# Five edits to the order of work in a recurrent attention segment: second scores moved up, tAB transposed in halves, fill transposed at the segment boundary, vA evacuated ahead of pS, one shared Wo pair traded for a Wv pair

## The chip, the cores and the metric

The kernel runs on one core of one Trainium2 chip. The metric is the device time of one execution in microseconds. The kernel before was timed three times.

## The reference

Two branches read the same `x` (2048 rows of 1024). Branch A is an attention with a small memory that is carried from segment to segment: 64 segments of 32 rows, 8 memory rows, 32 heads of 128. Branch B is a feed-forward block. A sigmoid gate mixes the two.

```
mem = mem0
for s in range(64):
    h = concat(mem, x[32*s : 32*s+32])                 # 40 rows x 1024
    q, k, v = h @ Wq, h @ Wk, h @ Wv                   # 32 heads of 128
    p = softmax(where(mask, q k^T / sqrt(128), -1e9))  # 40 x 40 a head
    o = (p v) @ Wo                                     # 40 x 1024
    mem = o[:8];  out[32*s : 32*s+32] = o[8:]
b = (gelu(x @ w_gate) * (x @ w_up)) @ w_down
return g * a + (1 - g) * b,   g = sigmoid((x * gate_w).sum(-1))
```

The memory rows make the segments a chain: segment s+1 cannot project its memory before Wo of segment s is done.

## The kernel before

The first three quarters of the time are the 64 segments, the rest is branch B, which the change leaves alone.

**Weights.** Each of Wq, Wk, Wv, Wo is cut into 16 pieces of 512 KB: 8 pieces (`i`) for each half of the heads (`u`). There is room for 50 of the 64 pieces. `PAIRS` names the indices whose two pieces (u = 0 and u = 1) share one slot; these 14 slots are loaded again in each segment, the others stay. `spent(k)` says that a piece has been used for the last time in the order of the walk, and issues the next load into its slot on SyncE's queue (SP). All reloads of a segment go through this one queue: first two Wk, two Wq and four Wv pieces near the start of the segment, then six Wo pieces during the first Wo pass. Wo pieces are read in strided form at first; `keep` writes them once into `wo_scr`, from where later loads are straight.

**Walk.** A segment is a fixed list of steps `(m, r, n)`: matrix m, round r (0 or 1, the half of the heads), place n. `HEAD` holds the first halves of k, q and v with pieces of the last Wo pass of the segment before in between; `BODY` is k, q of round 1, Wo of round 0 (`"o", 0`), v of round 1, and the first four Wo pieces of round 1 (`"o", 1`). `plan(s)` hangs all other work on these steps with `on(m, r, n, f)`; `f` runs ahead of that step. Each engine has one queue, which is worked off in the order in which `plan` and the walk emit it; waits are put in by a tracker of tiles (`_Prog`), which treats a PSUM bank as one thing and SBUF in cells of 64 bytes. Tiles share memory on purpose: stage `p` lies over `oRc` and `a_bf`, stage `q` over `qT`, `tAB` and `E8`, and `vA` and stage `o` over `oT`.

**One attention half.** `scores(u)` (PE lines 647 and 653, then DVE 659, 660, ACT 661, DVE 663 to 672) ends with the transpose `tAB` on DVE (line 672). `attend(u)` (PE lines 681 and 686) multiplies it with `vA`, the evacuated v. `take` copies the four result banks into `oT`, which Wo (line 735 in round 0, line 752 in round 1) reads. `trans` transposes a staged k or q on PE (`turn`, line 631, always into bank TT) and copies it back on DVE (line 617).

**Boundary.** `fold` (DVE lines 763, 764) adds the halves of Wo's result into `a_bf`, `next_mem` transposes this on PE (line 773) and copies it on DVE (line 776) into `hT`, the input of the next segment. `a_bf` is then written to `a_scr` by a DMA issued on GpSimd (POOL). PE is kept busy across the boundary by a fill or by `warm`, matmuls without a use.

**Fills.** Eight rows of each segment do not depend on the memory, so k, q and v of these rows are computed for four segments at once (`fill`, lines 789 and 799). `FILL` says which: after segments with s % 4 = 0 a k and a q, 1 a v and a q, 2 a v, 3 a k; they end with s = 58. A k or q fill is evacuated, transposed with `turn`, copied on DVE (line 821), and written to `qk_scr` by POOL (line 824). All writes to `qk_scr` share one lane, so each waits for the landing of the one before.

**Around the change.** In a segment s > 0 before, the first scores stand at `("k", 1, 0)`; ScalarE evacuates k of round 1 into stage `p` (`pS`, at `("q", 1, 1)`) and then v into `vA` (at `("q", 1, 3)`). At `("o", 0, 0)` stand the first `attend`, into banks B0, B1, B2 and SS, the transpose of `pS`, the q evacuation and the four takes (all on DVE); the second scores stand at `("o", 0, 6)`.

Of the kernel before, what the change touches and what calls it, by code (L numbers as in the profile page):

```python
# [210 lines left out]
def bass_gated_mix__memory_aug_recurrent_mem_tr__geglu_ffn__prompt_kernel(  # L211
# [34 lines left out]
    with ExitStack() as es:  # L246
# [133 lines left out]
        def keep(k):  # L380
# [5 lines left out]
        moved = {("o", 0, i): slots[home[h]] for i, h in zip(PAIRS["o"], (("k", 1, 2), ("k", 1, 3), ("k", 1, 4),  # L386
                                                                          ("q", 1, 6), ("q", 1, 7), ("v", 1, 4)))}
        nlane = [0]
# [238 lines left out]

        def turn(st):
            def f(e):
                for j in range(4):  # L630
                    ins = e.transpose(PBV[TT][:, j * 128:(j + 1) * 128], st[:, j * 128:(j + 1) * 128], ident[:, :])  # L631
                return ins
            op("pe", f, rd=[st.r(), ident.r()], wr=[BK(TT)])

        def trans(to, st):
            turn(stage[st])
            dve_copy(to[:, :, :, 0:32].rearrange("p j g c -> p (j g) c"),
                     PBV[TT][:, 0:512].rearrange("p (j g c) -> p (j g) c", g=4, c=32), [BK(TT)], [to.r()])

# [4 lines left out]
        def scores(u):  # L644

            def f(e):
# [24 lines left out]
               rd=[E8.r(), st8.r(8, 16)], wr=[pAB.r(256)])  # L671
            op("dve", lambda e: e.transpose(tAB[:, :], pAB[:, 0:512]), rd=[pAB.r()], wr=[tAB.r()], after=[fin])

        def attend(u, by=((2, "act"), (3, "dve"), (0, "act"), (1, "dve"))):
            bo = (B0, B1, B2, SS)

            def f(e):
                for j in range(4):
                    for g in range(4):
                        r = slice(32 * g, 32 * g + 32)  # L680
                        e.matmul(PB[bo[g]][:, j * LQ:(j + 1) * LQ], lhsT=vA[r, j, :],
                                 rhs=tAB[r, 64 * j:64 * j + LQ],
                                 start=(j == 0), stop=False, skip_group_check=True)
# [11 lines left out]
        def take(by):  # L695
            n = 4 * LQ
            for g, eng in by:
                b = (B0, B1, B2, SS)[g]
                cp[eng](oT[:, g, :, :].rearrange("p j c -> p (j c)"), PB[b][:, 0:n], [BK(b)], [oT.r(g * n, (g + 1) * n)])
# [8 lines left out]
        def proj(s, m, r, n):  # L708
# [14 lines left out]
            elif r == 0:  # L723
# [91 lines left out]

        def fill_put(m, u, G, st):
            if m == "v":
                return
            st = stage[st]
            turn(st)  # L820
            op("dve", lambda e: e.tensor_copy(st[:, :].rearrange("p (i x c) -> p x i c", i=4, x=16),
                                              PBV[TT][:, 0:512].rearrange("p (x i c) -> p x i c", x=16, i=4)), rd=[BK(TT)], wr=[st.r()])
            m4 = 3 * u if m == "q" else 1 + u
            op("pool", lambda e: e.dma_start(qk_scr[:, 4 * G:4 * G + 4, m4, :], st[:, :].rearrange("p (i y) -> p i y", i=4)),
               rd=[st.r()], wr=[("D", "qk", G, m, u)], lane="fq")
# [14 lines left out]
        def some(fs, n):  # L840
            return lambda: run(fs, n)
# [6 lines left out]
        def plan(s):  # L848
# [8 lines left out]
            def on(m, r, n, *fs, s=s):  # L857
                at.setdefault((s, m, r, n), []).extend(fs)

            if s == 0:  # L860
# [12 lines left out]
                on("k", 0, 4, gate)  # L873
                on("k", 0, 5, lambda: (firsts("v", 1), firsts("o", 0), firsts("o", 1)))
            if s % 4 == 3 and G < NG:
# [16 lines left out]
            if s == 0:  # L892
                on("k", 1, 1, lambda: attend(ua))
# [214 lines left out]
```

## Time and profile before

| | |
|---|---|
| runs (3) | 2383.08, 2384.80, 2384.88 us, median 2384.8 |
| profiled execution | 2371.4 us, span 2369.6 us |
| mean granted TensorE clock | 0.983 |
| PE busy | 2130.4 us, 90% of the span |
| DVE busy | 1044.7 us, 44% |
| ACT busy | 519.1 us, 22% |
| POOL busy | 432.9 us, 18% |
| DMA moved | 639.42 MB, mean 270 GB/s |

A segment takes some 25 us in the profile: segment 32 begins with its k projection at 927.27 us and the next at 952.75 us. The busy share of PE is a mean over stages and counts overlapping matmuls once, so what counts below is where PE stands idle inside a segment, and what ended that wait. The profiled execution was 13.4 us faster than the median of the runs.

### The profile page before, as it was taken

How to read it: one execution, taken by the hardware profiler on the slowest of the kernel's cores; microseconds unless marked ns; L12 is line 12 of the kernel's file. 1: busy time of each engine (PE TensorE's matmuls, PEld its weight loads, DVE VectorE, ACT ScalarE, POOL GpSimd, SP SyncE). 2: the span in 40 equal slices, each digit the busy share in tenths (PEclk: the TensorE clock that was granted, in tenths of full speed). 3: DMA queues.
4: the chain of work that ended last, by engine and by line, in shares of the span. 5: the costliest groups of instructions: out<-in, count | busy, mean ns of one | idle time of the engine just before them, and what ended most of it. 6: DMA issues, size and time to landing. Idle time of an engine off the chain costs nothing.

```text
span 2369.6 us, 74769 instructions
## 1 busy us (share of the span) xinstructions
PE 2130.4 (90%) x33827; PEld 1054.9 (45%) x33852; DVE 1044.7 (44%) x2438; ACT 519.1 (22%) x985; POOL 432.9 (18%) x821
## 2 busy tenths in 40 slices
PE   4588888989999998999899989988899999999999
PEld 2244444444444444444444444444464444444444
DVE  3344444444444444444444444444415436264463
ACT  1122222222222222222222222222103213032130
POOL 4322222222222222212222222222100000000000
PEclk9799999999999999999999999999999999999999
DMA  9979999989999999999899989999976260713530
GB/s 374 349 267 315 326 321 329 333 309 320 322 316 322 319 323 314 324 324 322 307 321 326 312 318 326 323 318 330 336 249 200 76 217 10 249 53 101 174 99 18
DMA packets 261453, 639.42 MB, mean 270 GB/s; under 512 B 28264, under 2 KB 102760, under 8 KB 261136
## 3 DMA queue, kind: packets, MB, share of 16 engines
q1 hardware_dynamic: 237312, 597.66, 72.4%
q0 software_dynamic: 13888, 26.31, 3.5%
q10 hardware_dynamic: 9936, 10.69, 1.3%
q8 instruction: 266, 4.36, 0.7%
q14 instruction: 51, 0.42, 0.0%
HBM read 596.85 MB, written 37.68 MB: 268 GB/s over the span
## 4 chain that ended last, share of the span: by engine, by line
PE 48%; DMA 29%; DVE 8%; issue 7%; ACT 5%; POOL 3%; ACTq 0%; SPq 0%; POOLq 0%
DMA a_scr<-a_bf 16%; PE pb L1009 14%; DMA wall<-wo_scr 6%; PE pb L719 6%; PE pb L1063 6%; PE pb L735 5%; PE pb L752 3%; PE pb L789 3%; DMA wall<-in_A_Wo_dram 2%; PE pb L960 2%; PE pb L1044 2%; PE pb L631 2%; PE pb L799 2%; ACT pS L614 1%; DMA xr_scr<-xr 1%
## 5 line engine op out<-in xcount | busy, mean ns | idle before, releaser
L719 PE MATMUL pb<-sl,hT 128*32 128x512 bf16 x12288 | 770.1, 382 | 7.2 <-issue 5.0
L719 PEld LDWEIGHTS pb<-sl,hT 128*32 128x32 bf16 x12288 | 342.4, 97 | 273.7 <-DVE hT L776 21.7
L789 PE MATMUL pb<-sl,hR 128*32 128x512 bf16 x3072 | 224.0, 393 | 9.2 <-issue 8.3
L1009 PE MATMUL pb<-xT,wg 128*128 128x512 bf16 x896 | 211.7, 379 | 0.7
L1009 PE MATMUL pb<-xT,wu 128*128 128x512 bf16 x896 | 211.7, 379 | 0.0
L752 PE MATMUL pb<-wall,oT 128*32 128x256 bf16 x4048 | 152.1, 276 | 38.0 <-DMA wall<-wo_scr 16.5
L763 DVE COPY part<-pb 64x256 f32<-64x256 f32 x128 | 54.0, 422 | 265.9 <-PE pb L752 263.4
L735 PE MATMUL pb<-wall,oT 128*32 128x512 bf16 x2048 | 153.1, 396 | 7.6 <-issue 0.2
L614 ACT ACTIVATE kS<-pb 128x512 bf16<-128x512 f32 x127 | 75.8, 597 | 367.9 <-PE pb L719 349.2
L617 DVE CAST oT<-pb 128x160 bf16<-128x160 f32 x382 | 105.5, 318 | 110.3 <-PE pb L686 110.3
L702 POOL COPY oRc<-oT 128x128 bf16<-128x128 bf16 x128 | 96.2, 752 | 313.3 <-DVE oT L617 311.9
L661 ACT ACTIVATE E<-pb 128x320 bf16<-128x320 f32 x128 | 56.0, 437 | 428.1 <-DVE pb L660 428.1
L1063 PE MATMUL pb<-wd,GT 128*128 128x512 bf16 x657 | 144.9, 379 | 2.1 <-DMA wd<-in_B_w_down_dram 1.2
L752 PEld LDWEIGHTS pb<-wall,oT 128*32 128x32 bf16 x4048 | 97.7, 97 | 93.8 <-issue 36.8
L1009 PEld LDWEIGHTS pb<-xT,wg 128*128 128x128 bf16 x896 | 87.0, 98 | 108.1 <-DVE GT L1025 3.7
L1017 ACT ACTIVATE s<-pb 128x512 f32<-128x512 f32 x112 | 66.7, 596 | 311.6 <-PE pb L1009 311.6
L1009 PEld LDWEIGHTS pb<-xT,wu 128*128 128x128 bf16 x896 | 87.5, 98 | 105.9
L1018 DVE SCALAR_TENSOR_TENSOR tp<-s,pb 128x512 f32<-128x512 f32 x112 | 77.0, 687 | 124.1 <-ACT s L1017 123.9
L659 DVE TENSOR_REDUCE st<-pb 128x8 f32<-128x320 f32 x128 | 62.9, 492 | 137.5 <-PE pb L653 137.5
L617 DVE COPY kT<-pb 128x512 bf16<-128x512 bf16 x128 | 53.7, 420 | 156.6 <-PE pb L631 156.6
L828 POOL COPY kT<-qkr 128x128 bf16<-128x128 bf16 x128 | 37.3, 291 | 451.6 <-DVE kT L617 389.3
L789 PEld LDWEIGHTS pb<-sl,hR 128*32 128x32 bf16 x3072 | 84.7, 99 | 68.6 <-issue 20.9
(93 smaller groups left out, 2249.9 us busy)
## 6 DMA issues: line engine op xcount, KB each, us to landing
wall<-wo_scr SPq DMA_DIRECT2D x336, 512.0 KB, 6.9
sl<-in_A_Wv_dram SPq DMA_DIRECT2D x268, 512.0 KB, 10.8
sl<-in_A_Wk_dram SPq DMA_DIRECT2D x142, 512.0 KB, 5.7
sl<-in_A_Wq_dram SPq DMA_DIRECT2D x142, 512.0 KB, 8.4
wd<-in_B_w_down_dram SPq DMA_DIRECT2D x42, 1024.0 KB, 5.5
wall<-in_A_Wo_dram SPq DMA_DIRECT2D x52, 512.0 KB, 7.9
wdF<-in_B_w_down_dram SPq DMA_DIRECT2D x7, 1024.0 KB, 7.7
wo_scr<-wall SPq DMA_DIRECT2D x12, 512.0 KB, 11.9
```

What stands on the lines that cost most here:

```text
L614: op("act", lambda e: e.activation(o, i, ACTF.Copy), rd=rd, wr=wr)
L617: op("dve", lambda e: e.tensor_copy(o, i), rd=rd, wr=wr)
L659: op("dve", lambda e: e.tensor_reduce(nm, sS, AX.X, ALU.max, negate=True), rd=[BK(SS)], wr=[st8.r(0, 8)])
L702: op("pool", lambda e: e.tensor_copy(oRc[:, :, 16 * u:16 * u + 16].rearrange("p c x -> p x c"), oT[:, :, :, 32:40].rearrange("p g j c -> p ...
L719: ins = e.matmul(PB[bk][32 * g:32 * g + 32, :], lhsT=h[:, i, :], rhs=w[:, g * 512:(g + 1) * 512], start=(n == 0), stop=(n == 7))
L735: ins = e.matmul(PB[XO][32 * g:32 * g + 32, :], lhsT=oT[:, j, x, 0:32], rhs=wall[:, na:nb + 1:nb - na, c:c + 256], start=(n == 0 and hp == 0),
L752: ins = e.matmul(PB[XO][32 * g:32 * g + 32, 256 * b:256 * b + 256], lhsT=oT[:, j, x, 0:32], rhs=w[:, c:c + 256], start=False, stop=(n % 4 ...
L789: ins = e.matmul(PB[b][32 * g:32 * g + 32, :], lhsT=h[:, k[2], :], rhs=w[:, g * 512:(g + 1) * 512], start=(n == 0), stop=(n == 7))
L1009: ins = e.matmul(PB[bk][:, 0:FB], lhsT=w[:, kc, cc:cc + 128], rhs=xT[:, :, :, kc, :].rearrange("p t i c -> p (t i) c"), start=(kc == 0), s ...
L1017: op("act", lambda e, hg=hg: e.activation(s1[:, :], hg, ACTF.Square, scale=SQ), rd=[BK(bg)], wr=[s1.r()])
L1018: op("dve", lambda e, hg=hg, t=t: e.scalar_tensor_tensor(out=t[:, :], in0=s1[:, :], scalar=1.0, in1=hg, op0=ALU.add, op1=ALU.mult), rd=[BK ...
L1063: ins = e.matmul(PB[bank[2 * k + hf]][:, :], lhsT=GT[:, j, tb * 128:(tb + 1) * 128], rhs=w[:, jj, hf * 512:(hf + 1) * 512], start=(j == 0) ...
```

## The change

- **Pairs.** Wo index 7 loses its shared slot and stays resident; Wv index 4 gets one. There are still 14 reloads in a segment: 2 Wk, 2 Wq, 5 Wv, 5 Wo. The fifth Wv reload is issued when piece 4 of v has been used in `HEAD`. The release of Wo slots in round 0 is spread differently (piece 0 after place 1; 1, 4 and 5 after place 3; 6 after place 5), and round 1 uses its pieces in the order 2, 3, 0, 1, 7, 4, 5, 6.
- **vA ahead of pS.** `vA` is evacuated at `("k", 1, 4)`. The first `attend` writes bank A0 in place of SS, its takes go to DVE (0, 3) and ACT (1, 2).
- **First scores** move from `("k", 1, 0)` to `("v", 0, 7)`, and the q transpose ahead of them goes one piece up, into bank A0. **Second scores** move from `("o", 0, 6)` to `("o", 0, 4)`, with their q transpose in bank SS.
- **tAB in halves.** The transpose of 512 columns becomes two of 256; `attend` becomes two operations, the first of which waits for the first half only.
- **Fill turned at the boundary.** The first fill of a segment is staged in `q` rather than `k`, its four transposes move from `("o", 1, 2)` to behind `fold(s, 0)`, into bank SS, and its DVE copy and its write to `qk_scr` to behind `next_mem(s, 0)`.

```diff
-        PAIRS = {"k": (0, 1), "q": (0, 1), "v": (0, 1, 2, 3), "o": (0, 1, 4, 5, 6, 7)}
+        PAIRS = {"k": (0, 1), "q": (0, 1), "v": (0, 1, 2, 3, 4), "o": (0, 1, 4, 5, 6)}
...
+            if m == "o":
+                return sorted(f + p, key=lambda i: i // 4)
...
-            op("dve", lambda e: e.transpose(tAB[:, :], pAB[:, 0:512]), rd=[pAB.r()], wr=[tAB.r()], after=[fin])
+            for c in (0, 256):
+                op("dve", lambda e, c=c: e.transpose(tAB[:, c:c + 256], pAB[:, c:c + 256]), rd=[pAB.r(c, c + 256)], wr=[tAB.r(c, c + 256)], after=[fin])
...
-            bo = (B0, B1, B2, SS)
+            bo = (B0, B1, B2, b3)
...
-            op("pe", f, rd=[vA.r(), tAB.r(), vB.r()], wr=[BK(b) for b in bo])
+            op("pe", f, rd=[vA.r(), tAB.r(0, 256)], wr=[BK(b) for b in bo])
+            op("pe", f2, rd=[tAB.r(256), vB.r()], wr=[BK(b) for b in bo])
...
-                    spent((*k[:2], i - 4))
-                    spent(k)
+                    for x in {1: (0,), 3: (1, 4, 5), 5: (2, 6), 7: (3, 7)}[n]:
+                        spent((*k[:2], x))
...
+        def fill_turn(m, st, bank=TT):
+            if m != "v":
+                turn(stage[st], bank)
+
-        def fill_put(m, u, G, st):
+        def fill_put(m, u, G, st, bank=None):
...
-            on("v", 0, 6, lambda: trans(qT, "q"))
+            on("v", 0, 5 if s else 6, lambda: trans(qT, "q", A0 if s else TT))
+            if s > 0:
+                on("v", 0, 7, lambda: scores(ua))
...
-            on(*(("k", 1, 1) if s == 0 else ("q", 1, 3)), lambda: evac(bank_of["v", 0], vA, "act"))
-            on("k", 1, 1 if s == 0 else 0, lambda: scores(ua))
+            on("k", 1, 1 if s == 0 else 4, lambda: evac(bank_of["v", 0], vA, "act"))
...
-                on("o", 0, 0, lambda: attend(ua, ((0, "dve"), (1, "dve"))))
-            on("o", 0, 0, lambda: trans(kT, "p" if s else "k"))
-            on("o", 0, 0, lambda: put_rest())
-            on("o", 0, 0, lambda: evac(bank_of["q", 1], stage["q"], "act"))
-            if s > 0:
-                on("o", 0, 0, lambda: take(((2, "dve"), (3, "dve"))))
-                on("o", 0, 0, lambda: rest_o(ua))
-            on("o", 0, 2, lambda: trans(qT, "q"))
-            on("o", 0, 6, lambda: scores(ub))
+                on("o", 0, 0, lambda: attend(ua, ((0, "dve"),), A0))
+                on("o", 0, 0, lambda: evac(bank_of["q", 1], stage["q"], "act"))
+                on("o", 0, 0, lambda: trans(kT, "p"))
+                on("o", 0, 0, lambda: put_rest())
+                on("o", 0, 0, lambda: take(((1, "act"), (2, "act")), A0))
+                on("o", 0, 2, lambda: trans(qT, "q", SS))
+                on("o", 0, 2, lambda: take(((3, "dve"),), A0))
+                on("o", 0, 2, lambda: rest_o(ua))
+                on("o", 0, 4, lambda: scores(ub))
...
-                on("o", 1, 0, lambda: fill_evac(*fl[0], A1, "k"))
-                on("o", 1, 2, lambda: fill_put(*fl[0], "k"))
+                on("o", 1, 0, lambda: fill_evac(*fl[0], A1, "q"))
...
             on("k", 0, 0, lambda: fold(s, 0), **nx)
+            if fl:
+                on("k", 0, 0, lambda: fill_turn(fl[0][0], "q", SS), **nx)
             on("k", 0, 0, some(f2, 4) if two else lambda: warm(5), **nx)
             on("k", 0, 0, lambda: next_mem(s, 0), **nx)
+            if fl:
+                on("k", 0, 0, lambda: fill_put(*fl[0], "q", SS), **nx)
```

More of the change, by code (lines that the diff above doesn't have):

```diff
@@ L626, in evac, with turn, trans @@
                 cp[how](t[:, :], PB[bank][:, :], [BK(bank)], [t.r()])
-        def turn(st):
+        def turn(st, bank=TT):
             def f(e):
                 for j in range(4):
-                    ins = e.transpose(PBV[TT][:, j * 128:(j + 1) * 128], st[:, j * 128:(j + 1) * 128], ident[:, :])
+                    ins = e.transpose(PBV[bank][:, j * 128:(j + 1) * 128], st[:, j * 128:(j + 1) * 128], ident[:, :])
                 return ins
-            op("pe", f, rd=[st.r(), ident.r()], wr=[BK(TT)])
-        def trans(to, st):
-            turn(stage[st])
+            op("pe", f, rd=[st.r(), ident.r()], wr=[BK(bank)])
+        def trans(to, st, bank=TT):
+            turn(stage[st], bank)
             dve_copy(to[:, :, :, 0:32].rearrange("p j g c -> p (j g) c"),
-                     PBV[TT][:, 0:512].rearrange("p (j g c) -> p (j g) c", g=4, c=32), [BK(TT)], [to.r()])
+                     PBV[bank][:, 0:512].rearrange("p (j g c) -> p (j g) c", g=4, c=32), [BK(bank)], [to.r()])
         sS = PB[SS][:, 0:320].rearrange("p (a c) -> p a c", a=8)
@@ L671, in scores, with attend @@
                rd=[E8.r(), st8.r(8, 16)], wr=[pAB.r(256)])
[L672 to L675 removed]
+            for c in (0, 256):
+                op("dve", lambda e, c=c: e.transpose(tAB[:, c:c + 256], pAB[:, c:c + 256]), rd=[pAB.r(c, c + 256)], wr=[tAB.r(c, c + 256)], after=[fin])
+        def attend(u, by=((2, "act"), (3, "dve"), (0, "act"), (1, "dve")), b3=SS):
+            bo = (B0, B1, B2, b3)
             def f(e):
@@ L680, in f, with f2 @@
                         r = slice(32 * g, 32 * g + 32)
-                        e.matmul(PB[bo[g]][:, j * LQ:(j + 1) * LQ], lhsT=vA[r, j, :],
-                                 rhs=tAB[r, 64 * j:64 * j + LQ],
-                                 start=(j == 0), stop=False, skip_group_check=True)
+                        ins = e.matmul(PB[bo[g]][:, j * LQ:(j + 1) * LQ], lhsT=vA[r, j, :],
+                                       rhs=tAB[r, 64 * j:64 * j + LQ],
+                                       start=(j == 0), stop=False, skip_group_check=True)
+                return ins
+            def f2(e):
                 for g in range(4):
@@ L693, in attend, with take @@
                 rest_o(u)
-        def take(by):
+        def take(by, b3=SS):
             n = 4 * LQ
             for g, eng in by:
-                b = (B0, B1, B2, SS)[g]
+                b = (B0, B1, B2, b3)[g]
                 cp[eng](oT[:, g, :, :].rearrange("p j c -> p (j c)"), PB[b][:, 0:n], [BK(b)], [oT.r(g * n, (g + 1) * n)])
@@ L814, in fill_evac @@
                 act_copy(st[:, :], PB[b][:, :], [BK(b)], [st.r()])
-        def fill_put(m, u, G, st):
+        def fill_turn(m, st, bank=TT):
+            if m != "v":
+                turn(stage[st], bank)
+        def fill_put(m, u, G, st, bank=None):
             if m == "v":
@@ L819, in fill_put @@
             st = stage[st]
-            turn(st)
+            if bank is None:
+                bank = TT
+                turn(st)
             op("dve", lambda e: e.tensor_copy(st[:, :].rearrange("p (i x c) -> p x i c", i=4, x=16),
-                                              PBV[TT][:, 0:512].rearrange("p (x i c) -> p x i c", x=16, i=4)), rd=[BK(TT)], wr=[st.r()])
+                                              PBV[bank][:, 0:512].rearrange("p (x i c) -> p x i c", x=16, i=4)), rd=[BK(bank)], wr=[st.r()])
             m4 = 3 * u if m == "q" else 1 + u
@@ L901, in plan @@
             if s > 0:
-                on("o", 0, 0, lambda: attend(ua, ((0, "dve"), (1, "dve"))))
-            on("o", 0, 0, lambda: trans(kT, "p" if s else "k"))
-            on("o", 0, 0, lambda: put_rest())
-            on("o", 0, 0, lambda: evac(bank_of["q", 1], stage["q"], "act"))
-            if s > 0:
-                on("o", 0, 0, lambda: take(((2, "dve"), (3, "dve"))))
-                on("o", 0, 0, lambda: rest_o(ua))
-            on("o", 0, 2, lambda: trans(qT, "q"))
-            on("o", 0, 6, lambda: scores(ub))
+                on("o", 0, 0, lambda: attend(ua, ((0, "dve"),), A0))
[7 more added lines that the diff above has]
+                on("o", 0, 4, lambda: scores(ub))
+            else:
+                on("o", 0, 0, lambda: trans(kT, "k"))
+                on("o", 0, 0, lambda: put_rest())
+                on("o", 0, 0, lambda: evac(bank_of["q", 1], stage["q"], "act"))
+                on("o", 0, 2, lambda: trans(qT, "q"))
+                on("o", 0, 6, lambda: scores(ub))
             on("v", 1, 0, some(f1, 3))
```

6 lines of the change are left out of this document (4 added, 2 removed).

## The prediction

> **What bounds the kernel now.** I read the page first, then the waits over the stretch 200 to 1715 us, which holds 60 of the 64 segments, then the order in time inside segment 32.
>
> ```profile
> PE 2130.4 (90%) x33827; PEld 1054.9 (45%) x33852; DVE 1044.7 (44%) x2438; ACT 519.1 (22%) x985; POOL 432.9 (18%) x821
> ...
> DMA a_scr<-a_bf 16%; PE pb L1009 14%; DMA wall<-wo_scr 6%; PE pb L719 6%; PE pb L1063 6%; PE pb L735 5%; PE pb L752 3%; PE pb L789 3%; DMA wall<-in_A_Wo_dram 2%; PE pb L960 2%; PE pb L1044 2%; PE pb L631 2%; PE pb L799 2%; ACT pS L614 1%; DMA xr_scr<-xr 1%
> ```
>
> The first line is of the page's engines, the second of its chain by line. PE is 90% busy, so only its idle tenth can be won. The chain runs 16% of the span through the small write of `a_bf` to `a_scr`, but what that write costs is only the part during which PE has nothing left to do. The waits say how much that is (columns: who waited for whom, us in total, times, longest):
>
> ```profile
> ACT pS L614 <- DMA a_scr<-a_bf: 92.0, 59, 3.6
> PE pb L681 <- ACT vA L614: 44.4, 54, 2.9
> PE pb L681 <- DVE tAB L672: 23.0, 48, 1.7
> PE pb L752 <- DMA wall<-wo_scr: 15.6, 27, 1.1
> ```
>
> Four places recur: the first attend (behind vA, itself behind pS, itself behind `a_scr`), the second attend (behind the transpose of tAB), Wo pieces that come late, and, in the rows below, the transpose of a staged fill between two groups of Wo. Each has one edit aimed at it. Segment 32 in time (start, duration, in brackets the idle time before it and what ended it):
>
> ```profile
> 939.41 0.60 ACT L614 ACTIVATE pS<-pb 128x512 bf16<-128x512 f32 x1 [2.31 <-DMA a_scr<-a_bf]
> 939.91 0.59 ACT L614 ACTIVATE vA<-pb 128x512 bf16<-128x512 f32 x1
> 940.55 0.27 PE L681 MATMUL pb<-tAB,vA 32*128 32x40 bf16 x16 [1.57 <-ACT vA L614]
> 942.28 1.05 PE L735 MATMUL pb<-wall,oT 128*32 128x512 bf16 x16
> 943.26 0.31 PE L647 MATMUL pb<-mS,ident 128*128 128x320 bf16 x1
> 944.79 1.93 PE L719 MATMUL pb<-sl,hT 128*32 128x512 bf16 x32
> 946.87 0.71 DVE L672 STREAM_TRANSPOSE tAB<-pAB 128x512 bf16<-128x512 bf16 x1
> 947.86 0.28 PE L681 MATMUL pb<-tAB,vA 32*128 32x40 bf16 x16 [0.49 <-DVE tAB L672]
> 948.60 0.62 PE L752 MATMUL pb<-wall,oT 128*32 128x256 bf16 x16
> 949.42 0.40 PE L631 MATMUL pb<-ident,kS 128*128 128x128 bf16 x4 [0.20 <-ACT kS L614]
> 949.75 0.40 PE L752 MATMUL pb<-wall,oT 128*32 128x256 bf16 x8
> 950.55 1.05 PE L789 MATMUL pb<-sl,hR 128*32 128x512 bf16 x16
> ...
> 951.25 0.42 DVE L764 TENSOR_TENSOR a_bf<-pb,part 64x256 bf16<-64x256 f32 x1
> 951.72 0.23 PE L773 MATMUL pb<-ident,a_bf 64*128 64x64 bf16 x2
> ```
>
> **A, vA ahead of pS.** Today the first attend starts 1.14 us after pS starts (939.41 to 940.55), because vA follows on the same queue, 0.50 us later. With vA done before, attend may follow pS itself, since it now writes bank A0, which pS has to empty first: the wait for `a_scr` stays, 0.50 us of it goes. The 54 waits total 44.4 us, mean 0.82, so most are longer than 0.50; at most 54 x 0.50 = 27 us goes. Short waits can only fall to zero, and a wait for tAB lies close under this one, so I take 22. Where a fill's q is staged in `oS`, under vA, vA must wait for its write to `qk_scr`. This write goes ahead of `a_scr` on the same POOL queue:
>
> ```profile
> 957.04 0.77 POOL L824 DMA_DIRECT2D qk_scr<-oS  x1 [0.19 <-issue]
> 957.81 0.55 POOL L938 DMA_DIRECT2D a_scr<-a_bf  x1
> qk_scr<-kS POOLq DMA_DIRECT2D x31, 128.0 KB, 3.8
> qk_scr<-oS POOLq DMA_DIRECT2D x31, 128.0 KB, 7.3
> a_scr<-a_bf POOLq DMA_DIRECT2D x64, 64.0 KB, 7.0
> qkr<-qk_scr POOLq DMA_DIRECT2D x65, 64.0 KB, 5.7
> sl<-in_A_Wv_dram SPq DMA_DIRECT2D x268, 512.0 KB, 10.8
> ```
>
> With the median landings in the last column, `oS` lands at 964.3 and `a_scr` at 964.8: vA slips in just ahead of pS and costs it nothing. If it did not, the 28 to 30 segments of this kind would lose the 0.50 each, 14 us; lower end of A therefore 8.
>
> **B, second scores two pieces up, tAB in halves.** Sixteen Wo matmuls take 0.98 us of PE's order (942.28 to 943.26), so the eight that are passed are 0.49 us. The second chain starts that much earlier, while PE's own work up to the second attend stays the same. The wait there is 23.0 / 48 = 0.48 us at the mean. The halves have no row in this trace. Two forms of one operation, 256 and 64 columns, bound them:
>
> ```profile
> L672 DVE STREAM_TRANSPOSE tAB<-pAB 128x512 bf16<-128x512 bf16 x121 | 86.1, 711 | 4.1
> L665 DVE TENSOR_TENSOR pAB<-E,st 128x256 bf16<-128x256 bf16 x120 | 51.0, 425 | 4.1
> L667 DVE TENSOR_TENSOR pAB<-E,st 128x64 bf16<-128x64 bf16 x120 | 26.2, 218 | 0.0
> ```
>
> 192 columns cost 207 ns, so 149 ns of each is fixed. With the same fixed part a half is 149 + (711 - 149) / 2 = 430 ns, the pair 860; without one, 356 and 711. I take 430, the price with a row behind it. The first half then comes 0.28 us sooner, the second 0.15 us later, and the second part of attend needs the second. So where DVE is last, only 0.49 - 0.15 = 0.34 us is won. 48 x 0.34 = 16, and some waits counted under other causes go too: 18 (ends 12, if half of the mean wait goes, and 23, the whole wait).
>
> [...]
>
> **C, fill turned at the boundary.** Before, the transpose splits Wo: the second Wo group starts at 949.75, 1.15 us after the first. Sixteen matmuls of that line issue in 0.44 us (the ones that follow, 8 in 0.22), so 0.71 us is spent on the transposes and the wait ahead of them. At the boundary the four transposes (0.33 us, 949.42 to 949.75) lie under `fold`, whose two DVE steps and their start take from 950.34, when the last Wo group starts, to 951.72:
>
> ```profile
> 950.34 0.40 PE L752 MATMUL pb<-wall,oT 128*32 128x256 bf16 x8 [0.19 <-DVE kS L821]
> 952.75 0.61 PE L719 MATMUL pb<-sl,hT 128*32 128x512 bf16 x8
> L821 DVE COPY kS<-pb 128x512 bf16<-128x512 bf16 x28 | 11.9, 425 | 35.3 <-PE pb L631 35.3
> ```
>
> That cover is 1.38 us, and PE fills it with 0.22 of Wo and 16 fill matmuls, 0.87: the transposes fit within 0.04 where a second fill runs. With 20 warm matmuls instead (1.08 us) they stick out by 0.25. 28 fills x 0.71 = 20, less 14 x 0.25 = 3.5: 16 us. Ends 11 (only the wait of 0.20 and 0.33 of transposes, less the 3.5) and 20. The DVE copy and the write to `qk_scr` come later, which is the third rival.
>
> **D, five Wo pieces instead of six, in the order of use.** Piece 1 was third in its queue and is second; 0 and 1 are needed first. Late Wo pieces cost 15.6 us in the waits above. I take 11, because a shorter segment brings the next need closer; ends 0 and 16.
>
> **E, what is late next.** The fifth Wv piece: the fourth of segment 32 is issued at 932.0 and takes 10.8 us, to 942.8. The rate when DMA is full gives 0.524 MB / 395 GB/s = 1.33 us for one more, 944.1.
>
> ```profile
> L378 SPq DMA_DIRECT2D sl<-in_A_Wv_dram x1: 518/518/518, 932.0 to 932.0; - x1
> DMA to landing us min/median/max: 10.8/10.8/10.8
> 912.00:915.00 3.00, 0.64 (x28) 0.20 (x20) 0.64 (x1) 1.08 (x2) 0.00 (x0) 1.00 1.01 395
> 953.00:955.00 2.00, 2.00 (x60) 1.46 (x56) 0.00 (x0) 0.00 (x0) 0.00 (x0) 1.00 0.56 123
> 934.48 0.54 POOL L494 DMA_DIRECT2D qkr<-qk_scr  x1 [0.29 <-POOL kT L828]
> ```
>
> v's last piece stands at about 944.79 + 7/8 x 1.73 = 946.3, with A 0.5 sooner: 1.7 us to spare here, 0.7 where `a_scr` takes its median 7.0 and not the 8.0 of this segment. The second scores need `qkr`, issued at 934.48, median landing 940.2; they would now stand near 942.3: also enough at the median, not in every segment. Queued behind either wait on PE is all the rest of the segment. Together between 0 and 61 x 0.5 = 30 us; I take 5, near the end that the spare time speaks for. The moved q transposes, the extra wait instructions and the takes on ACT lie beside PE's own work: nothing, or 0.1 us a segment (6 us) if they don't.
>
> **Sum.** 22 + 18 + 16 + 11 - 5 = 62 us. The profiled execution had 2371.4 us (span 2369.6), 13.4 below the median of the runs, 2384.8; against its own time that is 2309, and against the median 2323. The measurement can tell about 0.2%, 5 us, from no change.
>
> **Rivals.** *Weights become the bound.* For it: DMA is nearly full during each burst (share 1.01 at 395 GB/s), and a segment shorter by 1 us must move the same 14 pieces. PE's waits would move from vA and tAB to Wv and Wo: D falls to 0, E rises to 25 or more, gain 31 or less: about 2354. Against it: at the head of a segment the share is 0.56 at 123 GB/s, so there is slack between the bursts, and the burst lost from Wo is the one before that gap. *vA is not early*: A at 8, 2337; against it the two landings above. *The turned fill is written too late* (slower): the write of the staged fill now stands behind `next_mem` (951.72), its copy and its own DVE copy, so it starts at about 952.8, as the segment and its weight burst begin. If it takes the 7.3 us of `oS` and not the 3.8 of `kS`, it lands 7.4 us into the segment. After s % 4 = 0 the `oS` write shares its lane, and `a_scr` stands behind that on POOL: 957.04 is 4.3 us into the segment, so both slip by 3.1 us, 15 times, 47 us. After s % 4 = 3 the q evacuation, which overwrites stage `q`, slips too:
>
> ```profile
> 927.27 0.39 PE L719 MATMUL pb<-sl,hT 128*32 128x512 bf16 x4
> 933.09 0.60 ACT L614 ACTIVATE qS<-pb 128x512 bf16<-128x512 f32 x1 [0.27 <-PE pb L719]
> ```
>
> It starts 5.8 us into the segment, so it is 1.6 us late, 14 times, 22 us, and PE's transpose of q with it. 69 - 62 = 7 us slower, 2392; the mechanism decides from landings of 7.1 us on, and each us more costs 29. Against it: the start lies in the slack window of 123 GB/s, where 3.8 fits better.
>
> **How the numbers follow.** Forecast 2323 with 0.63 (2295 to 2340), weights 0.18, vA not early 0.10, the write too late 0.07, no effect 0.02. Ends of the terms added (8+12+11+0 to 27+23+20+16) with the costs give gains of some 1 to 86; the corners are unlikely together, so the range goes from 2292 to 2357, which leaves out the slower rival and the outer tails. Faster by over 0.2%: 0.63 + 0.18 + 0.10 = 0.91; within: 0.02; slower: 0.07.
>
> **What would show it.** A: attend starts some 0.7 us after pS starts, and its waits fall by half. B: the second attend's idle time near 0. C: no PE wait on a staged fill between Wo pieces; the write to `qk_scr` lands within 5 us. D: waits on `wall` mostly gone. Wrong if waits on Wv or on POOL's `kT` stand in their place, or if `a_scr` is issued later into its segment.

## The result, and the profile after

The changed kernel takes 2361.7 us in the median of 6 runs, the kernel before 2379.4 in 6: ratio 0.9947, 95% interval 0.9923 to 0.9971. That is faster by about 13 us, where 62 were forecast. (The medians alone differ by 18 us: three of the six runs of before are the earlier ones, 2383 to 2385 us, the other three have 2366 to 2376.) The profiled execution took 2364.5 us, span 2362.7.

The engines of the page after, and its chain by line:

```profile
PE 2148.5 (91%) x33852; PEld 1059.0 (45%) x33852; DVE 1026.3 (43%) x2440; ACT 544.1 (23%) x1111; POOL 434.6 (18%) x821
...
PE pb L726 15%; PE pb L1034 14%; DMA qk_scr<-oS 6%; PE pb L1088 5%; DMA qk_scr<-qS 5%; PE pb L796 5%; PE pb L742 5%; DMA sl<-in_A_Wv_dram 4%; PE pb L759 4%; DMA wall<-wo_scr 3%; PE pb L985 2%; PE pb L633 2%; PE pb L1069 2%; PE pb L806 2%; DMA xr_scr<-xr 1%
```

The write of `a_bf` to `a_scr`, 16% of the chain before, is no longer among these rows. The longest transfers in the chain are now the two writes of staged fills, 6% and 5%. Rows picked from the waits over 200 to 1715 us (who waited for whom, us in total, times, longest) say the same:

```profile
ACT vA L616 <- DMA qk_scr<-oS: 60.9, 28, 4.3
PE pb L684 <- ACT pS L616: 36.9, 27, 3.2
POOL qk_scr L837 <- DMA qk_scr<-qS: 19.7, 12, 2.5
ACT qS L616 <- DMA qk_scr<-qS: 16.3, 11, 2.8
PE pb L633 <- ACT qS L616: 14.7, 12, 2.5
PE pb L726 <- issue: 12.3, 15, 2.2
...
PE pb L726 <- DMA sl<-in_A_Wv_dram: 5.0, 11, 1.4
PE pb L759 <- DMA wall<-wo_scr: 4.6, 10, 1.6
...
PE pb L684 <- DVE tAB L675: 1.0, 1, 1.0
```

The wait for tAB went from 23.0 to 1.0 us and that for Wo from 15.6 to 4.6, as forecast. New are the third to fifth rows: a write to `qk_scr` and the q evacuation wait until the turned fill has been written from `qS`. Segment 53 (s % 4 = 1) in time; its k projection starts at 1439.22:

```profile
1438.55 0.41 DVE L834 COPY qS<-pb 128x512 bf16<-128x512 bf16 x1
1439.26 0.77 POOL L837 DMA_DIRECT2D qk_scr<-qS  x1 [2.34 <-DVE qS L834]
1439.66 0.85 SPq L380 DMA_DIRECT2D sl<-in_A_Wk_dram  x2
1444.89 0.77 POOL L837 DMA_DIRECT2D qk_scr<-oS  x1 [1.56 <-DMA qk_scr<-qS]
1445.66 0.55 POOL L963 DMA_DIRECT2D a_scr<-a_bf  x1
1453.86 0.60 ACT L616 ACTIVATE vA<-pb 128x512 bf16<-128x512 f32 x1 [4.33 <-DMA qk_scr<-oS]
1454.36 0.59 ACT L616 ACTIVATE pS<-pb 128x512 bf16<-128x512 f32 x1
1455.00 0.27 PE L684 MATMUL pb<-tAB,vA 32*128 32x40 bf16 x16 [1.99 <-ACT pS L616]
```

The write from `qS` is issued as the segment starts. The write from `oS` waits for its landing, `a_scr` stands behind that on POOL and goes out 6.4 us into the segment, where segment 33 of the kernel before had it 5.1 us in; the means of these segments are 6.57 and 5.11. That was one of the prediction's signs of being wrong. vA waits for `oS` and pS stands behind vA. PE waits 1.99 us at attend. In segment 56 (s % 4 = 0, starts at 1515.68) the q evacuation, which overwrites `qS`, waits for the same landing, and PE for it:

```profile
1516.15 0.78 POOL L837 DMA_DIRECT2D qk_scr<-qS  x1 [2.56 <-DVE qS L834]
1524.00 0.60 ACT L616 ACTIVATE qS<-pb 128x512 bf16<-128x512 f32 x1 [2.77 <-DMA qk_scr<-qS]
1524.65 0.61 PE L633 MATMUL pb<-ident,qS 128*128 128x128 bf16 x4 [2.54 <-ACT qS L616]
```

These are the two places of the prediction's third rival. Mean lengths of the segments 16 to 58 (from one k projection to the next, 10 or 11 segments each, in us) place the loss:

| kernel | s % 4 = 0 | 1 | 2 | 3 |
|---|---|---|---|---|
| before | 24.65 | 25.04 | 25.23 | 25.26 |
| after | 25.00 | 26.21 | 24.22 | 25.25 |
| e1_put_ahead | 24.60 | 24.87 | 24.38 | 24.88 |
| e2_own_lane | 24.92 | 24.23 | 24.47 | 25.11 |
| e3_fill_back | 24.45 | 24.65 | 24.18 | 24.80 |
| e4_fill_alone | 26.04 | 27.26 | 24.50 | 25.55 |
| e11_oS_on_ACT | 24.60 | 29.83 | 29.52 | 24.43 |

Segments of s % 4 = 2, with neither wait, became 1.0 us shorter, as much as the forecast's mean, 62 us over 61 segments, although C, 16 of the 62, has no part in them. Those of s % 4 = 1 became 1.2 us longer. Those of s % 4 = 3 have neither wait either and did not gain in this profile; in e1 to e3 they gained 0.15 to 0.46 us. Why they lag is not settled.

The table leaves out the first segments, and in this pair of profiles, which differ by only 6.9 us, the gain lies there. Segments 1 to 3 together are 11.0 us shorter than before, and segments 4 to 62 together 0.8 us longer. Segment 1 alone takes 26.0 to 27.4 us in the ten kernels of this document with the new pairs and 29.6 to 33.9 us in the seven with the old ones, 4.9 us less in the mean. In segment 1 of the kernel before (123.77 to 157.69 us) PE waits 6.9 us for Wo pieces that are still read in strided form; in e9_pairs_alone it waits 1.1 us for them. The row of the kernel before:

```profile
PE pb L752 <- DMA wall<-in_A_Wo_dram: 6.9, 2, 5.7
```

The pairs part also moves the first loads of Wo in segment 0 from `("k", 0, 5)` to `("v", 0, 5)`. Whether this or the one Wo reload less shortens segment 1 was not separated.

### The profile page after: what moved, and what is told of

Same layout as the page of the kernel before. It is cut to its first block, busy times and chain, and to the rows that moved or that the text cites. A ratio compares the mean times of both kernels' runs of the same rounds, so it can differ in the third digit from the quotient of the medians.

```text
span 2362.7 us, 74915 instructions
## 1 busy us (share of the span) xinstructions
PE 2148.5 (91%) x33852; PEld 1059.0 (45%) x33852; DVE 1026.3 (43%) x2440; ACT 544.1 (23%) x1111; POOL 434.6 (18%) x821
## 4 chain that ended last, share of the span: by engine, by line
PE 61%; DMA 26%; issue 4%; DVE 4%; ACT 3%; POOL 1%; SPq 0%; ACTq 0%; POOLq 0%
PE pb L726 15%; PE pb L1034 14%; DMA qk_scr<-oS 6%; PE pb L1088 5%; DMA qk_scr<-qS 5%; PE pb L796 5%; PE pb L742 5%; DMA sl<-in_A_Wv_dram 4%; PE pb L759 4%; DMA wall<-wo_scr 3%; PE pb L985 2%; PE pb L633 2%; PE pb L1069 2%; PE pb L806 2%; DMA xr_scr<-xr 1%
## 5 line engine op out<-in xcount | busy, mean ns | idle before, releaser
L726 PE MATMUL pb<-sl,hT 128*32 128x512 bf16 x12288 | 784.3, 385 | 21.9 <-issue 13.0
L726 PEld LDWEIGHTS pb<-sl,hT 128*32 128x32 bf16 x12288 | 347.2, 97 | 310.5 <-issue 36.1
L796 PE MATMUL pb<-sl,hR 128*32 128x512 bf16 x3072 | 221.3, 390 | 5.9 <-issue 5.3
L742 PE MATMUL pb<-wall,oT 128*32 128x512 bf16 x2048 | 158.9, 404 | 9.6 <-issue 2.9
L759 PE MATMUL pb<-wall,oT 128*32 128x256 bf16 x4056 | 143.4, 274 | 18.8 <-issue 7.1
L619 DVE CAST oT<-pb 128x160 bf16<-128x160 f32 x256 | 76.5, 320 | 143.6 <-PE pb L692 143.6
L616 ACT ACTIVATE qS<-pb 128x512 bf16<-128x512 f32 x189 | 112.9, 597 | 89.6 <-PE pb L692 50.9
L616 ACT ACTIVATE kS<-pb 128x512 bf16<-128x512 f32 x68 | 40.6, 597 | 360.2 <-PE pb L726 345.1
L616 ACT ACTIVATE vA<-pb 128x512 bf16<-128x512 f32 x128 | 76.2, 596 | 200.6 <-PE pb L726 135.3
```

The lines of the kernel that those rows point to most:

```text
L616: op("act", lambda e: e.activation(o, i, ACTF.Copy), rd=rd, wr=wr)
L619: op("dve", lambda e: e.tensor_copy(o, i), rd=rd, wr=wr)
L726: ins = e.matmul(PB[bk][32 * g:32 * g + 32, :], lhsT=h[:, i, :], rhs=w[:, g * 512:(g + 1) * 512], start=(n == 0), stop=(n == 7))
L742: ins = e.matmul(PB[XO][32 * g:32 * g + 32, :], lhsT=oT[:, j, x, 0:32], rhs=wall[:, na:nb + 1:nb - na, c:c + 256], start=(n == 0 and hp == 0),
L759: ins = e.matmul(PB[XO][32 * g:32 * g + 32, 256 * b:256 * b + 256], lhsT=oT[:, j, x, 0:32], rhs=w[:, c:c + 256], start=False, stop=(n % 4 ...
L796: ins = e.matmul(PB[b][32 * g:32 * g + 32, :], lhsT=h[:, k[2], :], rhs=w[:, g * 512:(g + 1) * 512], start=(n == 0), stop=(n == 7))
```

## The experiments

Two theories: W, the write of the turned fill lands too late; D, the weights bind the shorter segments. The runs, each beside the kernel before on the same chip:

| run | median us | before us | ratio, 95% interval |
|---|---|---|---|
| e1_put_ahead | 2330.5 | 2374.6 | 0.9818 (0.9780 to 0.9856) |
| e2_own_lane | 2331.2 | 2374.6 | 0.9823 (0.9798 to 0.9848) |
| e3_fill_back | 2328.9 | 2374.6 | 0.9812 (0.9776 to 0.9847) |
| e4_fill_alone | 2407.9 | 2374.6 | 1.0145 (1.0115 to 1.0175) |
| e5_A_back | 2330.4 | 2372.9 | 0.9824 (0.9803 to 0.9846) |
| e6_B_back | 2341.7 | 2372.9 | 0.9865 (0.9845 to 0.9886) |
| e7_tAB_whole | 2331.9 | 2372.9 | 0.9823 (0.9798 to 0.9848) |
| e8_pairs_back | 2355.1 | 2372.9 | 0.9921 (0.9894 to 0.9947) |
| e9_pairs_alone | 2362.1 | 2372.6 | 0.9958 (0.9935 to 0.9980) |
| e10_vA_alone | 2368.9 | 2372.6 | 0.9985 (0.9965 to 1.0005) |
| e11_oS_on_ACT | 2474.7 | 2372.6 | 1.0429 (1.0393 to 1.0464) |
| e12_without_C_and_A | 2340.8 | 2375.6 | 0.9857 (0.9821 to 0.9892) |
| e13_fill_alone_ahead | 2378.2 | 2376.6 | 1.0015 (0.9992 to 1.0039) |
| e14_scores_alone | 2366.6 | 2376.6 | 0.9955 (0.9933 to 0.9976) |
| e15_scores_and_vA | 2350.7 | 2376.6 | 0.9902 (0.9874 to 0.9931) |

Below, one thousandth of a ratio is taken as 2.4 us. The intervals make the difference of two runs uncertain by some 7 to 12 us, less between runs with the same kernel before beside them.

### The late write

**e1_put_ahead**

```diff
             on("k", 0, 0, lambda: fold(s, 0), **nx)
             if fl:
                 on("k", 0, 0, lambda: fill_turn(fl[0][0], "q", SS), **nx)
+            if fl:
+                on("k", 0, 0, lambda: fill_put(*fl[0], "q", SS), **nx)
             on("k", 0, 0, some(f2, 4) if two else lambda: warm(5), **nx)
             on("k", 0, 0, lambda: next_mem(s, 0), **nx)
-            if fl:
-                on("k", 0, 0, lambda: fill_put(*fl[0], "q", SS), **nx)
```

> The changed kernel with one step moved: the DVE copy of the turned fill and its write to qk_scr stand ahead of the boundary's matmuls and of next_mem, not behind them, some 0.9 us earlier. Theory W (the write of the staged fill lands too late and, through its lane, delays a_scr after s % 4 = 0, and through stage q delays the q evacuation after s % 4 = 3): segments of s % 4 = 1 took 26.21 us and those of s % 4 = 0 25.00 us in the changed kernel's profile, where s % 4 = 2, which have neither wait, took 24.22; the write starts at about 0.5 us before the segment, lands by about 4, a_scr is issued 5.1 us into the s % 4 = 1 segments again, and some 30 to 50 us go: 2310 to 2332. Theory D (the shorter segments are bound by the 14 weight pieces): the waits only change their name, 2355 to 2365.

Measured: 2330.5, 31 us below the changed kernel by ratio. One step some 0.9 us earlier wins more than twice what the whole change had won. W holds; by D nothing would have moved.

**e2_own_lane**

```diff
-               rd=[st.r()], wr=[("D", "qk", G, m, u)], lane="fq")
+               rd=[st.r()], wr=[("D", "qk", G, m, u)], lane="fo" if st is stage["o"] else "fq")
```

> The changed kernel, with a lane of its own for the qk_scr writes that are staged in oS, so that they no longer wait until the write staged in qS has landed; nothing else. Theory W: only the s % 4 = 1 segments recover, a_scr is issued at 5.1 us and not 6.6, these 15 segments go from 26.2 to about 24.3 us, 25 to 33 us in all: 2329 to 2337; the s % 4 = 0 segments stay at 25.0. Theory D: no change, 2355 to 2365.

Measured: 2331.2. The s % 4 = 1 segments are back at 24.23 us and those of s % 4 = 0 stay at 24.92. The wait in the lane is therefore nearly the whole loss: 15 segments by 1.98 us are 30 us, and the two kernels differ by 30 us by ratio. (The same segments take 24.65 to 24.87 us in e1 and e3, so the 1.98 is uncertain by some 0.5.)

**e3_fill_back**

```diff
-                on("o", 1, 0, lambda: fill_evac(*fl[0], A1, "q"))
+                on("o", 1, 0, lambda: fill_evac(*fl[0], A1, "k"))
+                on("o", 1, 2, lambda: fill_put(*fl[0], "k"))
```

(with both steps at the boundary taken out)

> The changed kernel with the first fill turned and written where it was before (stage k, inside the last Wo pass), all other parts kept. Theory W: both delays go (30 to 50 us), the 8 to 16 us that the turned fill gains go as well: 2320 to 2345. Theory D: the turned fill's gain goes and nothing comes back, 2365 to 2380.

Measured: 2328.9, the lowest of all, level with e1 and e2. Four of the five parts bring 45 us; the fifth, as it was made, takes 32 of them back.

**e4_fill_alone**, from the kernel before:

```diff
-                on("o", 1, 0, lambda: fill_evac(*fl[0], A1, "k"))
-                on("o", 1, 2, lambda: fill_put(*fl[0], "k"))
+                on("o", 1, 0, lambda: fill_evac(*fl[0], A1, "q"))
...
             on("k", 0, 0, lambda: fold(s, 0), **nx)
+            if fl:
+                on("k", 0, 0, lambda: fill_turn(fl[0][0], "q", SS), **nx)
...
             on("k", 0, 0, lambda: next_mem(s, 0), **nx)
+            if fl:
+                on("k", 0, 0, lambda: fill_put(*fl[0], "q", SS), **nx)
```

> The kernel before with this one part added: the first fill staged in q, turned at the boundary and written behind next_mem. Theory W: the delays come with this part alone; a_scr 1.5 us later in 15 segments (22 us), q evacuated late in 14 (10 to 20 us), less 8 to 16 us for the turned fill: slower than before by 15 to 35 us, some 2395 to 2415. Theory D: this part gains its 8 to 16 us by itself, some 2363 to 2372.

Measured: 2407.9, 34 us slower. The part loses the same 32 to 34 us in both kernels.

How long the write takes, in the issues of the changed kernel, of e1 and of e11 (KB each, median us to landing):

```profile
qk_scr<-oS POOLq DMA_DIRECT2D x31, 128.0 KB, 7.4
qk_scr<-qS POOLq DMA_DIRECT2D x31, 128.0 KB, 5.4
```

```profile
qk_scr<-qS POOLq DMA_DIRECT2D x31, 128.0 KB, 2.7
```

```profile
qk_scr<-oS ACTq DMA_DIRECT2D x28, 128.0 KB, 12.1
```

In the segments of s % 4 = 1, issued some 1.2 us ahead of the segment's first weight reload (e1) and not 0.4 us ahead of it, the same 128 KB land in half the time. That the reloads hold it up is argued from this order, not shown.

**e11_oS_on_ACT**

```diff
-            op("pool", lambda e: e.dma_start(qk_scr[:, 4 * G:4 * G + 4, m4, :], ...),
-               ..., lane="fq")
+            op("act" if st is stage["o"] and G > 1 else "pool", lambda e: e.dma_start(qk_scr[:, 4 * G:4 * G + 4, m4, :], ...),
+               ..., lane="fa" if st is stage["o"] and G > 1 else "fq")
```

> The kernel of e1_put_ahead with the qk_scr write of the second fill (staged in oS) issued on ScalarE's queue, with a lane of its own, in place of POOL's. a_scr no longer stands behind its 0.77 us on POOL, so in the 28 segments of s % 4 = 1 and 2 it is issued some 0.8 us earlier (4.3 and not 5.1 to 5.3 us into the segment). If a_scr and the write in oS bound these segments: 0.3 to 0.5 us each, 8 to 14 us, 2316 to 2322. If PE's own work and its stalls bound them by now: within 5 us of 2330.

Measured: 2474.7, a miss: some 145 us slower than e1. `a_scr` does go out earlier, 4.4 and 4.1 us into the two kinds of segment. But from ScalarE's queue the write takes 12.1 us, not 7.3, and in this kernel vA waits for it, with pS behind vA:

```profile
ACT vA L616 <- DMA qk_scr<-oS: 163.1, 28, 6.4
PE pb L684 <- ACT pS L616: 143.1, 38, 5.4
```

28 segments by some 5 us are 140 us. vA behind `oS` is the mechanism of the second rival; that pS waits behind vA makes it ten times as dear as the 0.50 us priced there.

### The other parts, one by one

**e5_A_back**, against e1:

```diff
-            on("k", 1, 1 if s == 0 else 4, lambda: evac(bank_of["v", 0], vA, "act"))
+            on(*(("k", 1, 1) if s == 0 else ("q", 1, 3)), lambda: evac(bank_of["v", 0], vA, "act"))
```

> The kernel of e1_put_ahead (all five parts, the staged write ahead of the boundary's matmuls) with vA evacuated behind pS again; attend keeps bank A0. By the prediction's term A: attend waits 0.5 us longer in most segments, about 22 us (8 to 27): 2338 to 2357 against the 2330 of e1_put_ahead. Rival (vA was not early, because it waits for the write staged in oS): 0 to 8 us in the half of the segments without that write, 2330 to 2338.

Measured: 2330.4, no loss. PE waits 36.7 us for vA here and 20.6 for pS in e1, but e1 waits more elsewhere (`L655 <- issue` 10.4 us for 6.6, `L796 <- issue` 7.2 for 3.4). The first attend starts 13.03 us into a segment in both kernels (mean of the four kinds). The profiled run of e1 was its slowest, 8 us above its median, so the longer issue waits may be that run's.

**e6_B_back**, against e1:

```diff
-                on("o", 0, 4, lambda: scores(ub))
+                on("o", 0, 6, lambda: scores(ub))
...
-            for c in (0, 256):
-                op("dve", lambda e, c=c: e.transpose(tAB[:, c:c + 256], pAB[:, c:c + 256]), ...)
+            op("dve", lambda e: e.transpose(tAB[:, :], pAB[:, 0:512]), ...)
```

> The kernel of e1_put_ahead with the second scores at piece 6 again and tAB transposed as one. By term B: the second attend waits 0.3 to 0.5 us again in most segments, 12 to 23 us: 2342 to 2353. Rival (the time only moves to the next late weight piece): 0 to 6 us, 2330 to 2336.

Measured: 2341.7, 11 us slower. **e7_tAB_whole**: of this diff the transpose alone.

> The kernel of e1_put_ahead with tAB transposed as one, the second scores staying up. The two halves took 0.77 us from start to end in the changed kernel's profile, the whole 0.71 before; the second attend now waits 0.05 us, so the whole one costs nothing there, and the first attend, where pS is last and not tAB, doesn't see it either: within 5 us of 2330. If the halves carry part of B, by the 0.28 us that the first half is earlier, 61 times: up to 17 us slower, 2347.

Measured: 2331.9, no difference. B's gain is the place of the scores. The halves in the changed kernel (busy us, mean ns):

```profile
L675 DVE STREAM_TRANSPOSE tAB<-pAB 128x256 bf16<-128x256 bf16 x240 | 92.5, 424 | 4.1
```

One takes 424 ns (430 were forecast), but the two overlap: 92.5 / 120 = 0.77 us a pair, not 0.86.

**e8_pairs_back**, against e1, with the order and the release of before:

```diff
-        PAIRS = {"k": (0, 1), "q": (0, 1), "v": (0, 1, 2, 3, 4), "o": (0, 1, 4, 5, 6)}
+        PAIRS = {"k": (0, 1), "q": (0, 1), "v": (0, 1, 2, 3), "o": (0, 1, 4, 5, 6, 7)}
...
-            if m == "o":
-                return sorted(f + p, key=lambda i: i // 4)
...
-                    for x in {1: (0,), 3: (1, 4, 5), 5: (2, 6), 7: (3, 7)}[n]:
-                        spent((*k[:2], x))
+                    spent((*k[:2], i - 4))
+                    spent(k)
```

> The kernel of e1_put_ahead with the pairs of before: six Wo and four Wv pieces, released and used in the old order. By the prediction's D less E: Wo pieces are late again (11 us, 0 to 16), Wv pieces no longer: 2330 to 2345, likeliest 2336. Rival (in the shorter segments the fifth Wv piece is the one that is late, so that the trade costs): 5 to 15 us faster, 2315 to 2325.

Measured: 2355.1, 25 us slower. PE's wait for Wo:

```profile
PE pb L757 <- DMA wall<-wo_scr: 40.4, 44, 2.7
```

In e1 this row has 2.5 us, in the kernel before 15.6: shorter segments need the same pieces sooner. **e9_pairs_alone**: the same diff, the other way round, on the kernel before.

> The kernel before with the pairs alone: five Wo and five Wv pieces, their new release and the new order of use. By e8_pairs_back (24 us slower without them, in the faster kernel): the late Wo pieces cost 14 to 16 us in the waits of before, so 10 to 16 us faster here, 2357 to 2363 against the 2373 of before, and waits on wo_scr nearly gone; the rest of the 24 us belongs to the shorter segments. By the prediction (11 less 5): about 2367.

Measured: 2362.1, 10 us faster. The trade is worth 10 us in the kernel before and 22 to 25 in the faster one. Some 5 us of each are the one segment 1 of the section above, so that the other segments gain some 5 and some 17 to 20.

**e10_vA_alone**, from the kernel before:

```diff
-            on(*(("k", 1, 1) if s == 0 else ("q", 1, 3)), lambda: evac(bank_of["v", 0], vA, "act"))
+            on("k", 1, 1 if s == 0 else 4, lambda: evac(bank_of["v", 0], vA, "act"))
...
-                on("o", 0, 0, lambda: attend(ua, ((0, "dve"), (1, "dve"))))
+                on("o", 0, 0, lambda: attend(ua, ((0, "dve"), (1, "dve")), A0))
...
-                on("o", 0, 0, lambda: take(((2, "dve"), (3, "dve"))))
+                on("o", 0, 0, lambda: take(((2, "dve"), (3, "dve")), A0))
```

> The kernel before with vA alone: evacuated ahead of pS, the first attend in bank A0. By the prediction's term A: 8 to 27 us faster, likeliest 2351. By e5_A_back (nothing lost without it): the wait for tAB and the write staged in oS take over, 0 to 8 us, 2365 to 2373.

Measured: 2368.9, 4 us faster, interval from 8 faster to 1 slower. The 44.4 us of waiting for vA are gone. Waits of PE at attend and of ScalarE at vA now:

```profile
ACT vA L614 <- DMA qk_scr<-oS: 24.2, 27, 2.1
PE pb L681 <- DVE tAB L672: 22.2, 47, 1.7
PE pb L681 <- ACT pS L614: 19.8, 29, 1.6
...
PE pb L681 <- issue: 11.6, 29, 1.6
```

The row for tAB is not new: it lies at the second attend, as before (23.0 us). What took the place of vA at the first attend are pS and, behind the row "issue", tAB: 26 of the 29 waits of that row are first attends that start 0.10 us after tAB is written, as in segment 43 (rows picked):

```profile
1216.41 0.71 DVE L672 STREAM_TRANSPOSE tAB<-pAB 128x512 bf16<-128x512 bf16 x1
1217.22 0.28 PE L681 MATMUL pb<-tAB,vA 32*128 32x40 bf16 x16 [0.32 <-issue]
```

**e12_without_C_and_A**: the diffs of e3 and e5 together.

> The changed kernel with the fill turned and written where it was before (as in e3_fill_back) and vA behind pS again (as in e5_A_back): what is left is the second scores and the halves, the first scores one step up with attend in bank A0, and the pairs. If neither the turned fill nor vA's place is worth anything here, as e5_A_back against e1_put_ahead and e1_put_ahead against e3_fill_back say: within 5 us of their 2329 to 2331. If each carries its term of the prediction (16 and 22 us) and only the scatter of runs hid it: 2345 to 2368.

Measured: 2340.8, between the two: 11 us lost against e3, where e5 lost nothing against e1. Whether the turned fill makes up for vA, or the scatter does, stays open.

**e13_fill_alone_ahead**: e4 with the diff of e1.

> The kernel before with the turned fill alone, its DVE copy and write ahead of the boundary's matmuls and of next_mem (e4_fill_alone with that one step moved). If e4_fill_alone lost its 33 us by the late write alone, term C is left: 11 to 20 us faster than before, 2353 to 2362. If the turned fill is worth nothing even with its write early (e1_put_ahead and e3_fill_back were equal): within 5 us of before, 2368 to 2378.

Measured: 2378.2, no difference from before. Its waits on Wo are longer than those of before (15.6 and 2.7):

```profile
PE pb L752 <- DMA wall<-wo_scr: 19.1, 31, 1.6
PE pb L752 <- DMA wall<-in_A_Wo_dram: 6.0, 6, 1.5
```

The shortest way from the second attend to the next segment did fall, from 4.53 to 4.15 us after s % 4 = 0 and from 4.12 to 3.85 after 3: 15 x 0.38 + 14 x 0.27 = 9 us, of which Wo pieces take 7 back.

**e14_scores_alone**: the changed kernel with the diffs of e3, e5 and e8. **e15_scores_and_vA**: with those of e3 and e8, so that vA stays ahead.

> The changed kernel with pairs, fill and vA as before: what is left is part B, the first scores one step up, the halves and attend in bank A0. By term B 12 to 23 us faster than before, 2350 to 2361; by e6_B_back (10 to 11 us lost without the second scores): about 2363; the first scores one step up take the wait of 0.31 us for tAB under the first attend as well, which vA's wait covers.

> e14_scores_alone with vA ahead of pS as well. If A is worth little in e10_vA_alone because tAB lies close under vA there, it shows here, where the scores are earlier: 10 to 20 us faster than e14_scores_alone. If it is worth little because PE's own stalls and the write staged in oS take the place of the wait for vA (as in e5_A_back): 0 to 6 us.

Measured: 2366.6, 11 us faster than before, and 2350.7, 13 us more. tAB had indeed hidden A: with the scores earlier, A is worth 13 us where it was worth 4, a difference close to the uncertainty, and tAB is no longer what the first attend waits for. PE's wait for tAB at attend and its longest remaining waits in e15:

```profile
PE pb L757 <- DMA wall<-wo_scr: 30.2, 35, 2.3
...
PE pb L682 <- ACT pS L614: 20.2, 29, 2.4
PE pb L724 <- issue: 10.8, 14, 1.9
...
PE pb L682 <- DVE tAB L673: 3.9, 4, 1.0
```

So the change adds up on the chip, in this order: B 10.8, A 12.7, the pairs 21.6 (e3 against e15), the turned fill -32.4 (the changed kernel against e3), 12.7 us together.

## Why the prediction was wrong

**The third rival was priced, and put aside.** Its two places, its lane and its order on POOL are what happened; it was given 0.07. The step that failed is the landing: 3.8 us, the median of `kS`, was taken as the likelier because the write would start in the slack at the head of the segment. It took 5.4, landing 5.2 us into the s % 4 = 1 segments and 6.4 into those of s % 4 = 0 (means of 11). And the rival was treated as a switch at 7.1 us, though by its own working `a_scr` is late from 4.3 us on: at 5.2 this is 0.9 us in 15 segments, 14 us, which belonged into the sum. It was 1.46 us, since POOL went on some 0.6 us after the landing, and the write from `oS`, vA and pS all moved with it: the first attend starts 14.58 us into these segments and 13.12 in e2, again 1.46. Each segment lost 1.98; the other 0.52 lie behind attend. There the granted TensorE clock is a part: in 4 of the 11 segments it is 0.5 for 3.4 us after PE's wait. From attend to the end these 4 take 12.05 us, the other 7 take 11.40, and those of e2 11.11. The rest is open. The q evacuation, 1.6 us late in the prediction's working, comes 0.6 us late by the same working with the landing at 6.4, 9 us in 14 segments; the 0.3 to 0.5 us between e2 and e1 or e3 are 4 to 7 us.

**A, 22 us forecast.** 4 alone, 13 on top of B, 1 to 11 when taken from the faster kernels. The 0.50 us a segment is right; but PE's wait at attend ends with the last of four things, and the row names only that one. With vA out of the way tAB, pS, the write from `oS` and PE's own stalls (rows "issue") came next, as the rows of e10_vA_alone show. The low end, 8, stood for the second rival, whose mechanism also worked: vA waits for `oS` 27 times in e10 and 28 in the changed kernel.

**B, 18 us.** 11 were measured: the place was right, the size too large, though the wait for tAB itself fell from 23.0 to 1.0 us. The second half cost 0.06 us (0.77 for the pair less 0.71 for the whole). The prediction had 0.15 from its 149 ns: the duration of one half does hold such a part, since 424 ns is 143 more than (711 - 149) / 2, but the two halves overlap.

**C, 16 us.** 0 even with the write early (e13, and e1 against e3), within the uncertainty. The transposes do lie under `fold` (at 900.47 to 900.87 us of e1, the two steps of `fold` at 900.59 to 901.47), but the term was too large: the way to the next segment became shorter by 0.38 and 0.27 us, where 0.71 and 0.46 went into the sum, so 9 us at best. In e13 the waits on Wo moved up and took most of this; in e1 they did not (2.5 us, 1.9 in e3), and what took it there is open.

**D less E, 6 us.** 10 alone, of which some 5 in segment 1, ahead of the stretch from which the prediction took its waits; 22 to 25 beside the rest. The weights rival is right for the old pairs: with them the shorter segments wait 30 to 40 us for Wo (e15, e8). E was right: 5.0 us of waits on Wv.

All but the late write together: 45 us (e3), where 62 less C's 16 makes 46. That is luck: A and B brought less than forecast, the pairs more. The ends 2295 and 2292 of the prediction lie 90 and 93 us below the median of 2384.8, more than the 86 us of all its terms together.

## What to carry over

Before a write is moved across a stage boundary, list who shares its semaphore lane, its queue and its buffer, and price each from the moment its landing passes the next use, as a term of the sum and not as a rival with a threshold. None of these waits was won by its whole row (44.4 us for vA, where A alone brought 4; 23.0 for tAB, where B brought 11; 40.4 for Wo in e8, where the pairs bring 25): look for the second-latest releaser in the same place, and take two waits that cover each other away together. Look at the first segments apart from the rest: what is won there is won once. In this kernel the order of the scarce transfers was worth more the shorter the segments became: the pairs 10 us alone, 22 to 25 beside the rest.

## What the runs showed of the hardware

**PE's instruction supply.** The rows "issue" are waits for nothing the profile shows. The page of the changed kernel lists a queue that fits (packets, MB, share):

```profile
q8 instruction: 266, 4.36, 0.7%
```

These are 266 packets of 16 KB. PE's two streams, 2 x 33852 instructions, are some 255 to a packet if these packets carry them and nothing else, an estimate from the two counts. Between 200 and 1650 us of e1, 54 of PE's 103 waits over 0.3 us end 1.15 to 1.55 us after such a packet has landed, 41 us in all; 6 would by chance. 52 of the 54 are rows "issue". In the kernel before it is 36 of 163, 27 us; 10 would by chance. No run took the supply away, so that it causes the stalls is inferred.

**The same write from two queues.** The write from `oS` lands after 7.3 us from POOL's queue (e1) and after 12.1 from ScalarE's (e11), issued some 0.4 us earlier into the segment. Why is not shown.

**The granted clock behind a long wait of PE.** In segment 53 of the changed kernel, behind the wait of 1.99 us, it is half (the last numbers are clock, DMA share and GB/s):

```profile
1455.75:1459.15 3.40, 3.33 (x57) 1.12 (x61) 1.09 (x4) 0.68 (x3) 1.04 (x2) 0.50 0.52 170
1455.82 1.04 PE L742 MATMUL pb<-wall,oT 128*32 128x512 bf16 x8
```

Eight Wo matmuls take 1.04 us there, as long as sixteen in the prediction's rows (1.05). In the kernel before and the changed kernel such stretches last 3.41 or 6.83 us between 200 and 1650 us, and the clock in them is 0.5. In the 17 profiles, between 200 and 1650 us, one begins during the wait or less than 2 us behind it for all 33 PE waits of 3 us or more, for 37 of 56 waits of 2 to 3 us, for 47 of 413 of 1 to 2 us, and for 32 of 1436 of 0.3 to 1 us. In segments 4 to 62 they add up to 14 us before, 44 in the changed kernel, 17 in e2 and 181 in e11. So a wait that is added to PE here may cost more than its own length: in the segments of s % 4 = 1 the first attend came 1.46 us later and each lost 1.98. That the wait lowers the clock is inferred from this order.
